# Turning tiles 0 to 3 once, with a copy kept by ScalarE, in an attention and gMLP mixer kernel

## The chip, the cores and the metric

The kernel runs on one core of a Trainium2 chip. The core has TensorE (PE, matrix products and transposes), VectorE (DVE), ScalarE (ACT), GpSimd (POOL) and SyncE (SP, which here issues DMAs). Each engine works through its own list of instructions in order; they meet only where one waits for another's result. TensorE writes its results to PSUM, a small memory of eight banks; a bank holds one tile of 128 x 512 fp32. The other working memory is SBUF. The metric is the device time of one execution in microseconds (us), the median of three.

## The reference

Input x is 2048 rows of 512. It is layer-normed to xn, and two branches read xn:

```python
s = attention(xn)      # 32 heads of 128; keys and values: the last 512 rows of a cache
z = gelu(xn @ w_in)    # 2048 x 1376, split in two halves of 688 columns
z1, z2 = z[:, :688], layernorm(z[:, 688:])
g = w_sp @ z2 + b_sp   # mixes the 2048 rows
out = x + s * silu((z1 * g) @ w_out)
```

All of it is fp32. The kernel gets that accuracy from three products: an operand is split into a high part, rounded to the faster matmul format fp32r, and a low part, which is the rest; high times high, high times low and low times high are added up in PSUM. In what follows a "rest" is the subtraction that makes a low part.

## The kernel before

**Tiles.** The 2048 rows of x are 16 tiles of 128 rows by 512. The first half, tiles 0 to 7, is loaded at the start into an SBUF array called `sacc`; this document is about those eight tiles. Each is layer-normed in place and then turned: four TensorE transposes of 128 x 128 (L215, for tile 0 at L231) put the turned tile in one PSUM bank (`flip`). From that bank ScalarE copies the high parts in two halves (L233), and VectorE subtracts to get the low parts (the rests, L59). The parts of tiles 0 to 3 lie in the blocks `X[0][h, 0]`, those of tiles 4 to 7 in `X[0][h, 1]`, h being the half of the 512 columns.

**Tile sums.** The query projections of most heads multiply a 2 x 2 arrangement of blocks with seven products in place of eight, in Strassen's manner. For that they need four combinations T1 to T4 of the turned tiles p and p + 4, for p = 0 to 3. They are made in two steps. When tile i of 4 to 7 is turned, ScalarE also copies the first 256 columns of its bank over the tile itself in `sacc` (y, L237), and VectorE subtracts them from the second 256 columns (L244). Later, in loop steps -3 to 0, `t_sums(p)` turns tile p a second time into a fresh bank, and `row_sums` has VectorE form three more combinations from that bank and y (L250 to L252). One step after each, `t_split(p)` splits the four results: high parts on ScalarE (L263), low parts on GpSimd.

**Order of the work.** The order is written out by hand, and every engine keeps the order in which the program emits its instructions. A prologue (L677 to L722) norms and turns tiles 0 to 3 and multiplies tiles 0, 1 and 2 with the first two of the four blocks of `w_in` (344 columns each); each product lands in a PSUM bank, is copied out by ScalarE into one of two staging tiles (L380) and stored to memory with a DMA that ScalarE issues (L381). I call these the z1 copies and stores. Then comes a loop over steps t from -7 on. Steps -7 to -4 turn one tile each, 4 to 7 (`ln_flip`); norm tile 6 or 7 ahead of need (L200, steps -7 and -6); and multiply one more tile with a block of `w_in` (`FILL`). All early steps carry a piece of the first query projections. From step 0 on each step also computes a block of attention scores (`score`). Work put in the list `late` runs at the end of its step, on VectorE, after all else of that step. `todo` holds what a step does besides, `t_sums` and `t_split` among it.

**Buffers.** PSUM is two pools of four banks: `ps_step` for what lives within a step and `ps_acc` for accumulators. Before the change all eight tiles are turned into banks of `ps_step`. SBUF scratch tiles of 128 x 512 named `rawx` come from the pool `xq` (five of them), which nothing else uses before step 30.

Of the kernel before, what the change touches and what calls it, by code (L numbers as in the profile page):

```python
# [8 lines left out]
F32 = mybir.dt.float32  # L9
# [3 lines left out]
OP = mybir.AluOpType  # L13
# [4 lines left out]
P = 128  # L18
# [3 lines left out]
NC = D // P  # L22
# [18 lines left out]
def mixer_kernel(ctx: ExitStack, tc: tile.TileContext, x, wh, w_in, w_sp, b_sp, w_out, out):  # L41
# [8 lines left out]
    nc = tc.nc  # L50
# [7 lines left out]
    def rest(engine, lo, whole, hi):  # L58
        engine.tensor_tensor(lo, whole, hi.bitcast(F32), op=OP.subtract)  # L59

    late = []
# [21 lines left out]
    ps_acc = psum.enter_context(tc.tile_pool(name="ps_acc", bufs=4, space=PSUM))  # L83
    ps_step = psum.enter_context(tc.tile_pool(name="ps_step", bufs=4, space=PSUM))
# [6 lines left out]
    xq = att.enter_context(tc.tile_pool(name="xq", bufs=5))  # L91
    sacc = sp.tile([P, T8, D], F32, name="sacc")


    def x8(shape, dtype=F32R):
        return xp.tile(shape, dtype, name="x8")
# [57 lines left out]
    X = {0: {}, 1: {}}  # L154

    def block():
        return x8([P, 2, 2, 512])

    def quarter(t, j):
        return t[:, :, j * P:(j + 1) * P]  # L160
# [31 lines left out]
    def ln_open(i):  # L192
        a, b = next(g for g in GROUPS if g[0] <= i < g[1])
        if i == b - 1:
            ln_stats([sacc[:, j, :] for j in range(a, b)], a)

    def ln_apply(t, i):
        mean, r = rx[i]
        if i:
            nc.vector.scalar_tensor_tensor(t, t, mean, r.to_broadcast([P, D]), op0=OP.subtract, op1=OP.mult)  # L200
        else:
            for k in range(2):
                sl = t[:, k * (D // 2):(k + 1) * (D // 2)]
                nc.vector.tensor_scalar(sl, sl, mean, r, op0=OP.subtract, op1=OP.mult)
# [7 lines left out]
    def flip(t, late=False):  # L212
        ps = ps_acc.tile([P, NC, P], F32, name="ps_a") if late else ps_step.tile([P, NC, P], F32, name="ps_3")
        for c in range(NC):
            nc.tensor.transpose(ps[:, c, :], t[:, c * P:(c + 1) * P], ident)  # L215
        return ps

    def ln_flip(i, parts=1):
        n, j = divmod(i, 4)
        if j == 0:  # L220
            for h in range(2):
                X[0][h, n] = block()
        if parts == 1:
            ps = flip(sacc[:, i, :])
        else:
            ps = ps_step.tile([P, NC, P], F32, name="ps_3")
        rests, rest_of = [], []
        for h in range(2):
            if parts > 1:
                for c in (2 * h, 2 * h + 1):  # L230
                    nc.tensor.transpose(ps[:, c, :], sacc[:, i, c * P:(c + 1) * P], ident)  # L231
            hi, lo = (quarter(X[0][h, n][:, a], j) for a in range(2))
            nc.scalar.copy(hi, ps[:, 2 * h:2 * h + 2])  # L233
            rests.append((lo, ps[:, 2 * h:2 * h + 2], hi))
        if n == 1:
            p2, y = ps.rearrange("p c q -> p (c q)"), sacc[:, i, :]
            nc.scalar.copy(y[:, :256], p2[:, :256])  # L237
            rest_of.append((y[:, 256:], p2[:, 256:], y[:, :256]))
        if parts > 1:
            return rests  # L240
        for r in rests:
            rest(nc.vector, *r)
        for r in rest_of:
            nc.vector.tensor_tensor(*r, op=OP.subtract)  # L244

    TS = ("T2", "T1", "T3", "T4")

    def row_sums(ps, y, o):

        nc.vector.tensor_tensor(o[:, :256], y[:, :256], ps[:, :256], op=OP.subtract)  # L250
        nc.vector.tensor_tensor(o[:, 256:], ps[:, :256], y[:, 256:], op=OP.add)
        nc.vector.tensor_tensor(y[:, :256], ps[:, 256:], o[:, 256:], op=OP.subtract)  # L252

    def t_sums(p):
        if p == 0:
            X[0].update((k, block()) for k in TS)
        row_sums(flip(sacc[:, p, :]).rearrange("p c q -> p (c q)"), sacc[:, 4 + p, :], sacc[:, p, :])

    def t_split(p):
        y, o = sacc[:, 4 + p, :], sacc[:, p, :]  # L260
# [110 lines left out]
    def z1_product(i, n, between=lambda: None):  # L371
        ps = ps_acc.tile([P, 512], F32, name="ps_a") if n or i >= T8 else ps_step.tile([P, 512], F32, name="ps_3")
        zmm(ps[:, :NB], i, n, range(2))
        between()
        zmm(ps[:, :NB], i, n, range(2, NC))
        return ps

    def z1_out(i, n, ps):
        z = zs.tile([P, NB], F32, name="z1")
        nc.scalar.copy(z, ps[:, :NB])  # L380
        nc.scalar.dma_start(z1_dram[:, i, n * NB:(n + 1) * NB], z)  # L381

    def z1_piece(i, n, between=lambda: None):
        z1_out(i, n, z1_product(i, n, between))
# [186 lines left out]
    def at(t, f, *args):  # L571
        todo.setdefault(t, []).append((f, args))
# [52 lines left out]
                q_events.setdefault(t0 + done + 2, []).append((q_done, g, k))  # L625

    for p in range(4):
        at(-3 + p, t_sums, p)
        at(-2 + p, t_split, p)
    ends = {}  # L630
    ends.setdefault(-2, []).append((keep_x, (0, 1)))
# [48 lines left out]
    low0 = split_piece(w0, 0, None, True), split_piece(w0, 1, None, True)  # L680
    ln_apply(rows[0], 0)
    low = ln_flip(0, 2)
    ln_open(1)
    for r in (*low0, *low):
# [4 lines left out]
    ps = ps_step.tile([P, 512], F32, name="ps_3")  # L689
    zmm_in(FIRST, ps[:, :NB], 0, 0, 0, 10)  # L690
    ln_open(2)
    ln_flip(1)
    zmm_in(FIRST, ps[:, :NB], 0, 0, 10, 12)
    low1 = [split_piece(w1, k, None, True) for k in range(4)]
# [3 lines left out]
    ps = ps_step.tile([P, 512], F32, name="ps_3")  # L698
# [6 lines left out]
    ps = ps_acc.tile([P, 512], F32, name="ps_a")  # L705
    zmm_in(THIRD, ps[:, :NB], 0, 1)
    ln_flip(2)
    ln_apply_late(3)
    ln_open(4)
# [4 lines left out]
    rest(nc.vector, *lowq)  # L714
    z1_out(0, 1, ps)
    z1_out(1, 1, ps1)
    ln_apply(rows[4], 4)
    ln_apply(rows[5], 5)
    z1_piece(2, 0)
    ln_open(6)  # L720
    ln_open(7)
    z1_piece(2, 1)  # L722

    FILL = dict(zip((-7, -6, -5, -4, -3, -2, -1, 0, 1, 8),
                    [(i, 1) for i in range(3, T8)] + [(i, 0) for i in range(4, T8)] + [(3, 0)]))
# [2 lines left out]
    for t in range(T0, T1):  # L728
# [6 lines left out]
        i = t + XL  # L735
# [23 lines left out]
        if t in DRAIN:  # L759
            ps = z1_product(*DRAIN[t])  # L760
# [21 lines left out]
    ps = z1_product(*LAST[-1])  # L782
# [422 lines left out]
```

## Time and profile before

| | us |
|---|---|
| Median of three runs | 1763.73 |
| Lowest and highest | 1763.12, 1763.81 |
| The profiled execution | 1763.41 |
| Its span in the profile | 1761.6 |

| Engine | Busy, us | Instructions |
|---|---|---|
| TensorE, matmuls | 1754.7 | 8463 |
| TensorE, weight loads (beside the matmuls) | 1506.7 | 8463 |
| VectorE | 1491.0 | 2470 |
| GpSimd | 1226.6 | 1151 |
| ScalarE | 1186.7 | 2621 |

The prologue and steps -7 to 0 take the first 46 us of the span. Rows of the profile name a line of the kernel, an engine, an operation and tiles as "out<-in"; "x4" merges four in a row; text in brackets is how long the engine had been idle before, and whose result it waited for. Matmuls are pipelined: the recorded time of one overlaps the next, so what a matmul holds of TensorE is the distance from its start to the next start. ACTq rows are DMAs that ScalarE issues; they take time on ScalarE's list though they do not count as busy.

### The profile page before, as it was taken

The numbers are of one execution on the slowest core, as the hardware profiler recorded it, in microseconds if no ns is written. First come the engines' busy times: TensorE is split into PE (matmuls) and PEld (weight loads), VectorE is DVE, ScalarE is ACT, GpSimd is POOL, SyncE is SP. The second block draws the span as 40 slices with busy tenths as digits, with TensorE's granted clock in tenths as the row PEclk, the third lists the DMA queues.
The fourth block names the chain that finished last, engine by engine and source line by source line (L and its number), as shares of the span: only waits on it lengthen the run. The fifth ranks groups of instructions, "written<-read, shape, count | busy, mean of one in ns | idle before, by whom it ended". The sixth has DMA issues, their size and how long they took to land.

```text
span 1761.6 us, 28515 instructions
## 1 busy us (share of the span) xinstructions
PE 1754.7 (100%) x8463; PEld 1506.7 (86%) x8463; DVE 1491.0 (85%) x2470; ACT 1186.7 (67%) x2621; POOL 1226.6 (70%) x1151
## 2 busy tenths in 40 slices
PE   9999999999999999999999999999999999999999
PEld 8888888888888888888888888888888899999997
DVE  6789989898998989988888888888888647887875
ACT  5777777777777777777777777777777546543333
POOL 2889888888888889878888888888888411000032
PEclk9999999999999999999999999999999999999999
DMA  5688887888888889787887877877788652655496
GB/s 203 209 236 253 247 248 233 248 240 236 251 241 239 250 231 272 217 262 223 224 224 221 229 227 220 226 222 219 232 226 247 216 194 86 224 187 177 148 257 206
DMA packets 171708, 394.25 MB, mean 224 GB/s; under 512 B 23840, under 2 KB 53792, under 8 KB 152352
## 3 DMA queue, kind: packets, MB, share of 16 engines
q1 hardware_dynamic: 166944, 386.80, 74.8%
q10 hardware_dynamic: 4608, 5.64, 0.9%
q8 instruction: 66, 1.08, 0.3%
q14 instruction: 90, 0.74, 0.1%
HBM read 229.55 MB, written 162.79 MB: 223 GB/s over the span
## 4 chain that ended last, share of the span: by engine, by line
PE 98%; DMA 1%; DVE 0%; ACT 0%; issue 0%; SPq 0%; ACTq 0%
PE ps_a L473 17%; PE ps L65 13%; PE ps L67 13%; PE ps L66 13%; PE ps L906 11%; PE ps_a L540 6%; PE ps_a L539 6%; PE ps_a L538 6%; PE ps_a L67 2%; PE ps_a L66 2%; PE ps_a L65 2%; PE ps_f L67 1%; PE ps_f L66 1%; PE ps_f L65 1%; PE ps_f L906 1%; DMA pL<-p_dram 1%
## 5 line engine op out<-in xcount | busy, mean ns | idle before, releaser
L59 POOL TENSOR_TENSOR pT_l<-pL,pT_h 128x512 fp32r<-128x512 f32 x507 | 658.0, 1301 | 185.1 <-ACT pT_h L530 176.1
L502 ACT ACTIVATE prob<-ps,nm 128x512 f32<-128x512 f32 x512 | 354.0, 691 | 339.7 <-DVE nm L500 331.6
L562 DVE SCALAR_TENSOR_TENSOR sacc<-ps,sums,sacc 128x512 f32<-128x512 f32 x496 | 369.8, 746 | 119.2 <-PE ps L67 114.0
L473 PE MATMUL ps_a<-x,x 128*128 128x512 f32 x1266 | 365.3, 389 | 0.0
L511 DVE STREAM_TRANSPOSE pL<-prob 128x512 f32<-128x512 f32 x512 | 358.8, 701 | 0.5 <-ACT prob L502 0.4
L500 DVE TENSOR_REDUCE nm<-ps 128x1 f32<-128x512 f32 x512 | 340.3, 665 | 3.0 <-PE ps L67 2.9
L530 ACT CAST pT_h<-pL 128x512 fp32r<-128x512 f32 x512 | 318.4, 622 | 9.2 <-ACT z L380 4.2
L473 PEld LDWEIGHTS ps_a<-x,x 128*128 128x128 f32 x1266 | 237.7, 188 | 49.2 <-issue 0.2
L59 POOL TENSOR_TENSOR wl<-raw,wh 128x512 fp32r<-128x512 f32 x186 | 241.7, 1299 | 10.9 <-ACT wh L145 10.9
L65 PE MATMUL ps<-wh,qT_h 128*128 128x512 f32 x512 | 199.7, 390 | 0.3 <-DVE sacc L562 0.2
L538 PE MATMUL ps_a<-pT_h,wh 128*128 128x512 f32 x512 | 199.9, 390 | 0.0
L67 PE MATMUL ps<-wh,qT_l 128*128 128x512 f32 x512 | 199.6, 390 | 0.0
L540 PE MATMUL ps_a<-pT_l,wh 128*128 128x512 f32 x512 | 199.4, 389 | 0.0
L65 PE MATMUL ps<-wh,oT_h 128*128 128x512 f32 x512 | 199.3, 389 | 0.0
L66 PE MATMUL ps<-wl,qT_h 128*128 128x512 f32 x512 | 199.3, 389 | 0.0
L539 PE MATMUL ps_a<-pT_h,wl 128*128 128x512 f32 x512 | 199.3, 389 | 0.0
L67 PE MATMUL ps<-wh,oT_l 128*128 128x512 f32 x512 | 199.2, 389 | 0.0
L66 PE MATMUL ps<-wl,oT_h 128*128 128x512 f32 x512 | 199.2, 389 | 0.0
L906 PE MATMUL ps<-b,x 128*128 128x344 f32 x1248 | 191.8, 316 | 0.0
L906 PEld LDWEIGHTS ps<-b,x 128*128 128x128 f32 x1248 | 191.5, 188 | 0.0
L59 POOL TENSOR_TENSOR b<-b 128x512 fp32r<-128x512 f32 x2 | 2.5, 1292 | 189.5 <-DMA x<-s_dram 189.5
L59 POOL TENSOR_TENSOR x<-wq,x 128x256 fp32r<-128x256 f32 x177 | 131.1, 741 | 0.0
(216 smaller groups left out, 3039.5 us busy)
## 6 DMA issues: line engine op xcount, KB each, us to landing
p_dram<-pL SPq DMA_DIRECT2D x128, 1024.0 KB, 4.7
pL<-p_dram SPq DMA_DIRECT2D x256, 192.0 KB, 4.0
raw<-wh SPq DMA_DIRECT2D x188, 256.0 KB, 6.1
pL<-p_dram SPq DMA_DIRECT2D x256, 128.0 KB, 4.0
x<-w_sp SPq DMA_DIRECT2D x24, 1024.0 KB, 5.1
pL<-p_dram SPq DMA_DIRECT2D x256, 64.0 KB, 3.9
wq<-wh SPq DMA_DIRECT2D x60, 256.0 KB, 5.6
z_dram<-z ACTq DMA_DIRECT2D x32, 172.0 KB, 3.3
```

Of the source, the lines that this page charges most:

```text
L59: engine.tensor_tensor(lo, whole, hi.bitcast(F32), op=OP.subtract)
L65: nc.tensor.matmul(ps, lh, rh, start=first, stop=False)
L66: nc.tensor.matmul(ps, lh, rl, start=False, stop=False)
L67: nc.tensor.matmul(ps, ll, rh, start=False, stop=last)
L473: nc.tensor.matmul(qps[g, bank], wt["q", g, k][a][:, c * P:(c + 1) * P], X[g * 2 // H][ORDER[k]][:, b, c], start=first, stop=r == 5, skip_ ...
L500: nc.vector.tensor_reduce(nm, ps, axis=AX.X, op=OP.max, negate=True)
L502: nc.scalar.activation(prob[t], ps, AF.Exp, bias=nm, accum_out=sums[b][:, j:j + 1])
L511: nc.vector.transpose(pL[b][:, :, j * P:j * P + P].rearrange("p a (c q) -> p a c q", q=Q), prob.pop(t).rearrange("p (a c q) -> p a c q", a ...
L530: nc.scalar.copy(h, p)
L538: nc.tensor.matmul(pps[b], vh, ph, start=c == 0, stop=False)
L562: nc.vector.scalar_tensor_tensor(at, ps, rs, at, op0=OP.mult, op1=OP.add)
L906: nc.tensor.matmul(ps, a, b, start=k != "P4" and c == 0 and m == 0, stop=c == RP - 1 and m == 2, skip_group_check=True)
```

## The change

Tiles 0 to 3 are turned only once, in the prologue. The bank of each is kept until ScalarE has copied it whole into a `rawx` tile (`keep_whole`): the copy of tile 0 stands after the z1 copies of tiles 0 and 1, that of tile 1 in the middle of the next product, those of tiles 2 and 3 in the middle of the one after. In ScalarE's list this is: two z1 copies, copy 0, copy 1, z1 copy, copy 2, copy 3, z1 copy. Tiles 0 and 1 are turned into banks of `ps_acc` now.

The combinations are formed when tile p + 4 is turned, in steps -7 to -4: `ln_flip` puts `row_sums` into `late`, four subtractions that read the bank of tile p + 4 and the kept copy of tile p. So the bank of tile p + 4 stays in use until the end of its step, and the four subtractions of a pair stand together. The second turning and the old sums in steps -3 to 0 are gone; what is left at step -3 allocates the blocks for T1 to T4. `t_split` stays where it was. DMAs are neither added nor removed.

```diff
+    def keep_whole(i):
+        p2, whole[i] = whole[i], xq.tile([P, 512], F32, name="rawx")
+        nc.scalar.copy(whole[i], p2)
...
         if parts == 1:
-            ps = flip(sacc[:, i, :])
+            ps = flip(sacc[:, i, :], i == 1)
         else:
-            ps = ps_step.tile([P, NC, P], F32, name="ps_3")
-        rests, rest_of = [], []
+            ps = ps_acc.tile([P, NC, P], F32, name="ps_a")
+        rests = []
...
+        p2 = ps.rearrange("p c q -> p (c q)")
         if n == 1:
-            p2, y = ps.rearrange("p c q -> p (c q)"), sacc[:, i, :]
+            y = sacc[:, i, :]
             nc.scalar.copy(y[:, :256], p2[:, :256])
-            rest_of.append((y[:, 256:], p2[:, 256:], y[:, :256]))
+            late.append((row_sums, p2, y, sacc[:, i - 4, :], whole[i - 4]))
+        whole[i] = p2
...
-    def row_sums(ps, y, o):
-
-        nc.vector.tensor_tensor(o[:, :256], y[:, :256], ps[:, :256], op=OP.subtract)
-        nc.vector.tensor_tensor(o[:, 256:], ps[:, :256], y[:, 256:], op=OP.add)
-        nc.vector.tensor_tensor(y[:, :256], ps[:, 256:], o[:, 256:], op=OP.subtract)
-
-    def t_sums(p):
-        if p == 0:
-            X[0].update((k, block()) for k in TS)
-        row_sums(flip(sacc[:, p, :]).rearrange("p c q -> p (c q)"), sacc[:, 4 + p, :], sacc[:, p, :])
+    def row_sums(ps, y, o, x):
+
+        for to, x0, x1 in ((y[:, 256:], ps[:, 256:], y[:, :256]), (o[:, :256], ps[:, :256], x[:, :256]),
+                           (o[:, 256:], ps[:, 256:], o[:, :256]), (y[:, :256], x[:, 256:], o[:, 256:])):
+            nc.vector.tensor_tensor(to, x0, x1, op=OP.subtract)
+
+    def t_blocks():
+        X[0].update((k, block()) for k in TS)
...
     for p in range(4):
-        at(-3 + p, t_sums, p)
+        if p == 0:
+            at(-3, t_blocks)
         at(-2 + p, t_split, p)
...
     z1_out(1, 1, ps1)
+    keep_whole(0)
     ln_apply(rows[4], 4)
     ln_apply(rows[5], 5)
-    z1_piece(2, 0)
+    z1_piece(2, 0, lambda: keep_whole(1))
     ln_open(6)
     ln_open(7)
-    z1_piece(2, 1)
+    z1_piece(2, 1, lambda: (keep_whole(2), keep_whole(3)))
```

More of the change, by code (lines that the diff above doesn't have):

```diff
@@ L216, in flip @@
         return ps
+    whole = {}
+    def keep_whole(i):
+        p2, whole[i] = whole[i], xq.tile([P, 512], F32, name="rawx")
+        nc.scalar.copy(whole[i], p2)
     def ln_flip(i, parts=1):
@@ L242, in ln_flip @@
             rest(nc.vector, *r)
-        for r in rest_of:
-            nc.vector.tensor_tensor(*r, op=OP.subtract)
     TS = ("T2", "T1", "T3", "T4")
-    def row_sums(ps, y, o):
-        nc.vector.tensor_tensor(o[:, :256], y[:, :256], ps[:, :256], op=OP.subtract)
-        nc.vector.tensor_tensor(o[:, 256:], ps[:, :256], y[:, 256:], op=OP.add)
-        nc.vector.tensor_tensor(y[:, :256], ps[:, 256:], o[:, 256:], op=OP.subtract)
-    def t_sums(p):
-        if p == 0:
-            X[0].update((k, block()) for k in TS)
-        row_sums(flip(sacc[:, p, :]).rearrange("p c q -> p (c q)"), sacc[:, 4 + p, :], sacc[:, p, :])
+    def row_sums(ps, y, o, x):
[4 more added lines that the diff above has]
+        X[0].update((k, block()) for k in TS)
     def t_split(p):
```

## The prediction

> **What bounds the kernel now.** I read the page first: the busy times and the chain that ended last.
>
> ```profile
> span 1761.6 us, 28515 instructions
> PE 1754.7 (100%) x8463; PEld 1506.7 (86%) x8463; DVE 1491.0 (85%) x2470; ACT 1186.7 (67%) x2621; POOL 1226.6 (70%) x1151
> PE 98%; DMA 1%; DVE 0%; ACT 0%; issue 0%; SPq 0%; ACTq 0%
> ```
>
> TensorE is the bound: busy for 1754.7 of 1761.6 us and 98% of the chain. A busy TensorE can still hide waits, so I asked next what it waited for, over the whole span:
>
> ```profile
> PE ps L673 <- POOL ident masks.py:199: 1.3, 1, 1.3
> PE ps L231 <- ACT x L233: 0.5, 1, 0.5
> PE ps L368 <- DVE pT_l L59: 0.3, 1, 0.3
> PE ps L65 <- DVE sacc L562: 0.2, 1, 0.2
> ```
>
> Four waits, 2.3 us in all, and none near the code that changes. So TensorE work that is taken out shortens the run by what it holds of TensorE's time, unless a new wait takes its place. The rest of the working is therefore TensorE's timeline around the change, and the timelines of ScalarE and VectorE beside it.
>
> **What is removed on TensorE.** The loop steps -3 to 0 each begin with a second turning of one of tiles 0 to 3 (four 128x128 transposes at L215). First the group over the whole span and in the window 33.2 to 43 us, then TensorE's timeline; its columns are start, duration, engine, line.
>
> ```profile
> L215 PE MATMUL ps<-ident,sacc x44: 271/272/328, 9.6 to 42.7; 128*128 128x128 f32 x44
> ...
> L215 PE MATMUL ps<-ident,sacc x16: 271/272/273, 33.2 to 42.7; 128*128 128x128 f32 x16
> 33.25 0.60 PE L215 MATMUL ps<-ident,sacc 128*128 128x128 f32 x4
> 33.60 0.40 PE L65 MATMUL ps_a<-wh,x 128*128 128x344 f32 x1
> 33.84 0.32 PE L66 MATMUL ps_a<-wl,x 128*128 128x344 f32 x1
> 34.00 0.32 PE L67 MATMUL ps_a<-wh,x 128*128 128x344 f32 x1
> 42.33 0.60 PE L215 MATMUL ps<-ident,sacc 128*128 128x128 f32 x4
> ```
>
> All 16 of these go. A recorded duration (272 ns) is not what a transpose holds, since neighbours overlap: four of them occupy TensorE from 33.25 to the next start at 33.60, 0.35 us. The matmul behind them then takes 0.24 us to the next start (33.60 to 33.84) where its neighbour takes 0.16 (33.84 to 34.00), so the switch costs another 0.08. One turning is worth 0.43 to 0.44 us, four are worth **1.75 us**. No transpose is added: tiles 0 to 7 are turned in the prologue and in steps -7 to -4 as before.
>
> [...]
>
> **What is added on ScalarE.** Four copies of a whole turned tile, 128x512 from PSUM. The same operation stands later in this kernel, and around the new place ScalarE's timeline reads:
>
> ```profile
> L320 ACT COPY rawx<-ps_a x8: 578/578/580, 166.8 to 571.5; 128x512 f32<-128x512 f32 x8
> 18.59 0.33 ACTq L381 DMA_DIRECT2D z_dram<-z  x1
> 18.95 0.45 ACT L380 COPY z<-ps_a 128x344 f32<-128x344 f32 x1 [0.40 <-ACT z L380]
> 19.43 0.33 ACTq L381 DMA_DIRECT2D z_dram<-z  x1
> 20.47 0.45 ACT L380 COPY z<-ps 128x344 f32<-128x344 f32 x1 [1.07 <-DMA z_dram<-z]
> 21.37 0.45 ACT L380 COPY z<-ps_a 128x344 f32<-128x344 f32 x1 [0.45 <-PE ps_a L67]
> 22.22 0.65 ACT L233 CAST x<-ps 128x256 fp32r<-128x256 f32 x2 [0.40 <-ACT z L380]
> 22.75 0.39 ACT L237 COPY sacc<-ps 128x256 f32<-128x256 f32 x1
> 24.80 0.65 ACT L233 CAST x<-ps 128x256 fp32r<-128x256 f32 x2 [0.69 <-PE ps L215]
> 26.70 0.45 ACT L380 COPY z<-ps_a 128x344 f32<-128x344 f32 x1 [0.97 <-PE ps_a L67]
> ```
>
> The copies cost 4 x 0.58 = 2.3 us of ScalarE, less an overlap of about 0.09 each (two casts of 0.37 take 0.65 together). I laid them out in program order. The z1 store issue at 19.43 ends at 19.76. Copy 0 runs from 19.79 to 20.37, copy 1 to 20.86. The z1 copy now at 20.47 follows at 20.77, its store issue ends at 21.58, copies 2 and 3 run to 22.68, the z1 copy now at 21.37 moves to 22.59, and its store issue ends at 23.40. Tile 4's casts, now at 22.22, start at 23.43: **ScalarE is 1.2 us late there**. The idle time at 24.80 and 26.70 absorbs it: tile 5's casts come 0.3 us late (the z1 copy between ends at 24.71, its store issue at 25.07), and the copy at 26.70 is on time again. The only DMAs moved are those three z1 stores, 0.3 to 1.2 us later; the pair of staging tiles has them landed again by about 25.3 (1.9 us after issue: the copy at 20.47 waits for the store at 18.59), before the copy at 26.70 wants one.
>
> Who waits for tile 4's casts? VectorE's rests, and behind them TensorE's product of tile 4.
>
> **What moves on VectorE.** The 16 small subtractions stay 16 (four per pair of tiles), but 12 move from steps -3 to 0 into steps -7 to -4, where each group stands at the end of its step, ahead of the next tile's rests.
>
> ```profile
> 23.17 0.76 DVE L59 TENSOR_TENSOR x<-ps,x 128x256 fp32r<-128x256 f32 x2 [0.28 <-ACT sacc L237]
> 23.85 0.41 DVE L244 TENSOR_TENSOR sacc<-ps,sacc 128x256 f32<-128x256 f32 x1
> 24.18 0.74 DVE L200 SCALAR_TENSOR_TENSOR sacc<-sacc,mv,rs_r 128x512 f32<-128x512 f32 x1
> 25.76 0.76 DVE L59 TENSOR_TENSOR x<-ps,x 128x256 fp32r<-128x256 f32 x2 [0.84 <-ACT sacc L237]
> 31.81 0.76 DVE L59 TENSOR_TENSOR x<-ps,x 128x256 fp32r<-128x256 f32 x2 [1.94 <-ACT sacc L237]
> 34.23 0.69 DVE L775 SCALAR_TENSOR_TENSOR qT_l<-ps_a,qT_h 128x512 fp32r<-128x512 f32 x1 [1.33 <-ACT qT_h L400]
> 34.84 0.41 DVE L250 TENSOR_TENSOR sacc<-sacc,ps 128x256 f32<-128x256 f32 x1
> 35.17 0.42 DVE L251 TENSOR_TENSOR sacc<-ps,sacc 128x256 f32<-128x256 f32 x1
> 35.62 0.42 DVE L252 TENSOR_TENSOR sacc<-ps,sacc 128x256 f32<-128x256 f32 x1
> ```
>
> An independent subtraction follows after 0.33 us (34.84 to 35.17), one that reads its predecessor after 0.45 (35.17 to 35.62). The new four have two such dependences: 0.33 + 0.45 + 0.45 + 0.33 = 1.56 us. A step with rests (0.68), a layer-norm apply (0.66) and sums (1.56) fills 2.90 us of VectorE; the steps without the apply take 2.24. TensorE's step is 3.03 us (33.25 to 42.33 is three of them). VectorE keeps pace, with little to spare.
>
> The consumers are the third matmul of each tile's product, which reads the first rest (24.92, 27.95, 30.97; the row at 19.25 is for the next part):
>
> ```profile
> 19.25 0.32 PE L65 MATMUL ps_a<-wh,x 128*128 128x344 f32 x1
> ...
> 24.52 0.40 PE L65 MATMUL ps_a<-wh,x 128*128 128x344 f32 x1
> 24.92 0.32 PE L67 MATMUL ps_a<-wh,x 128*128 128x344 f32 x1
> 27.95 0.32 PE L67 MATMUL ps_a<-wh,x 128*128 128x344 f32 x1
> 30.97 0.32 PE L67 MATMUL ps_a<-wh,x 128*128 128x344 f32 x1
> ```
>
> Tile 4: the rests start once ScalarE's last copy of the bank has ended, as the row at 23.17 shows, so at 24.38; the first ends at 24.80, wanted at 24.92. Tile 5: rests 24.38, apply 25.06, sums 25.72 to 27.28, next rests 27.28, first done 27.70, wanted 27.95. Tile 6: 30.18, done 30.60, wanted 30.97. Tile 7: 32.42, done 32.84, wanted after 33.6. Every margin is positive, the tightest 0.12 us. I take **no stall**, and keep 0 to 1.0 us: at the lower end the margins hold; at the upper all of ScalarE's added 2.3 us arrives at tile 4's first rest, which had 1.33 us in hand (it ends at 23.17 + 0.42, the time of one such operation, = 23.59, and is wanted at 24.92).
>
> [...]
>
> **New claims on buffers.** Turned tiles 0 to 3 hold a PSUM bank until their copy. Tiles 0 and 1 now draw from the pool of accumulators, and the product of tile 2 with the second weight block, which starts at 19.25, is its fifth allocation. If buffers went strictly round, it would take tile 0's bank and wait for copy 0. The rows above say otherwise: the product at 33.60 is the ninth allocation of that pool and would take the bank of the fifth, which VectorE reads until 34.92; it didn't wait. Banks go by order of release, and the first released are those of the two z1 copies before the store issues at 18.59 and 19.43. So no wait: 0, with 1.17 us as the upper end (copy 0's end at 20.37, plus 0.05 for the signal, less 19.25).
>
> **Does the gain survive?** From step 0 on TensorE only reaches its later work 1.75 us sooner. GpSimd is the busiest helper there:
>
> ```profile
> 40.86 1.31 POOL L59 TENSOR_TENSOR wl<-raw,wh 128x512 fp32r<-128x512 f32 x1 [0.93 <-ACT wh L145]
> 53.68 1.30 POOL L59 TENSOR_TENSOR wl<-raw,wh 128x512 fp32r<-128x512 f32 x1 [1.74 <-ACT wh L145]
> ```
>
> It works without a gap from 40.86 to 51.93. That stretch starts about 0.9 us earlier (two turnings precede it), so it ends at 51.05; the next request comes at 51.93. TensorE has only the 0.2 us wait behind it. The gain stays, and if GpSimd were late it could take back at most the 1.75.
>
> **Sum.** -1.75 + 0 + 0 = -1.75 us: the profiled run of 1763.41 us (span 1761.6 and 1.8 around it) becomes 1761.7, and the median of 1763.73, which lies 0.3 above that run, becomes **1762.0**.
>
> **Rivals.**
> 1. Strictly round buffers: TensorE loses 1.17 us at 19.25 and gains 0.58 net, 1763.1. Against it speaks 33.60.
> 2. Late rests: one stall of up to 1.0 us in steps -6 to -4, 1762.1 to 1763.0. For it speaks the margin of 0.12; against it, that a delay of TensorE widens every later margin.
> 3. The gain is given back to GpSimd or to loads between 43 and 70 us: no change, 1763.7. Against it, TensorE's empty list of waits there.
> 4. Slower: VectorE becomes the bound of steps -7 to -4. It decides where a new subtraction costs over 0.63 us in place of 0.39 (the long steps then take 3.86 us and the short ones 3.20, and two long and one short lose 2 x 0.83 + 0.17, less the margin of 0.12: the gain). At the most a row allows, the 0.69 of an operation twice as wide (34.23), the long steps take 4.10 and the short ones 3.44: 2 x 1.07 + 0.41 - 0.12 = 2.4 lost, +0.7 net, 1764.4. Against it, 0.33 to 0.45 in the rows.
> 5. Each transpose is worth its recorded duration: 16 x 0.272 = 4.35 us, 1759.4. Against it, four in 0.35 us. [...]
>
> **How the numbers follow.** My forecast has a chance of 0.68; the rivals 0.09, 0.11, 0.05, 0.04 and 0.03. The forecast's own range, with 0.3 us of spread between runs, is 1761.7 to 1762.4. Rivals 1 and 2 stretch the range up to 1763.5; 1761.0 below leaves room for a turning that holds about 0.2 us more than I read. About 0.2% (3.5 us) is what a measurement of this kernel tells from no change: faster is below 1760.2, slower above 1767.3. Only rival 5 is surely faster, and I add 0.01; rival 4 as priced stays within, so slower has 0.03 for a cause that I don't see, and 0.93 is left for the same.
>
> **What would show it.** After the change: 28 transposes of L215 instead of 44 before 43 us; the L215 rows gone between steps -3 and 0, with TensorE steps of about 2.6 us there; the wait list of TensorE as before; tile 4's casts at about 23.4 us and its rests at 24.4; VectorE without subtractions of tile sums after 36 us; the first score matmul, now 0.35 us after 42.33, at about 40.9. A TensorE wait on a ScalarE copy at 19.25 is rival 1, one on L59 between 24.9 and 31 is rival 2 or 4. A first score at 40.9 with a total unchanged is rival 3.

## The result, and the profile after

The changed kernel takes **1775.09 us** (median of 6 runs, 1774.00 to 1775.67) against 1763.77 us for the kernel before (6 runs, 1763.12 to 1764.40). The ratio is 1.0065 with a 95% interval of 1.0055 to 1.0075: **slower by 11.3 us**, where 1762.0 was predicted. The profiled execution took 1775.42 us, with a span of 1773.6. One run of experiment 8 below took 2197.6 us at a granted clock of 0.753 and is not counted; every other run lies at 0.997 to 1.000.

The page of the changed kernel, span and busy times:

```profile
span 1773.6 us, 28485 instructions
PE 1762.5 (99%) x8447; PEld 1514.3 (85%) x8447; DVE 1491.6 (84%) x2470; ACT 1188.2 (67%) x2625; POOL 1226.3 (69%) x1151
```

TensorE issues 16 instructions fewer, as it should, and yet is busy for 7.8 us longer (1762.5 against 1754.7) and idle for 4.2 us more (11.1 against 6.9). So there are two losses, idle time and work that takes longer. The list of TensorE's waits names the first:

```profile
PE ps L912 <- ACT b L826: 4.1, 1, 4.1
PE ps L678 <- POOL ident masks.py:199: 1.3, 1, 1.3
...
PE ps_a L67 <- DVE x L59: 0.2, 1, 0.2
```

The last row, 0.2 us, is dealt with further below. One wait of 4.1 us is new: L912 for L826. (Lines below the edit have moved: L912 is L906 of the kernel before, L826 is L820, L258 stands in place of L244 and L250 to L252.) L912 is the row mixing, the product with `w_sp`: 1344 matmuls of 344 columns that start some 1450 us after the changed code. L826 is the gelu of the last z products, the stage just before. TensorE's timeline there, first of the kernel before, then of the changed one (columns: start, duration, engine, line, in brackets the idle time before):

```profile
1489.00 0.32 PE L67 MATMUL ps_a<-raw,x 128*128 128x344 f32 x1
1489.15 22.24 PE L906 MATMUL ps<-b,x 128*128 128x344 f32 x144
1511.23 1.08 PE L906 MATMUL ps_f<-b,x 128*128 128x344 f32 x6
```

```profile
1488.01 0.31 PE L67 MATMUL ps_a<-raw,x 128*128 128x344 f32 x1
1492.41 25.60 PE L912 MATMUL ps<-b,x 128*128 128x344 f32 x144 [4.09 <-ACT b L826]
1517.85 7.42 PE L912 MATMUL ps_f<-b,x 128*128 128x344 f32 x46
```

Until 1488 us the changed kernel is ahead by 0.99 us (1489.00 less 1488.01). Then it waits for the last gelu. Before, the row mixing did not: ScalarE's timelines of the kernel before and the changed one show that the same gelu ran at 1492.55 there, 3.4 us after the row mixing had begun.

```profile
1492.55 0.80 ACT L820 ACTIVATE b<-ps_a 128x344 f32<-128x344 f32 x2
```

```profile
1489.04 1.81 ACT L847 ACTIVATE b<-b,rz_r 128x688 f32<-128x688 f32 x2 [2.61 <-POOL rz_r L841]
1490.88 0.77 ACT L853 CAST b<-b 128x688 fp32r<-128x688 f32 x1
1491.56 0.80 ACT L826 ACTIVATE b<-ps_a 128x344 f32<-128x344 f32 x2
```

The wait is not all. The next table has the granted clock by stretches (columns: stretch, its length, then busy time and count of PE, PEld, DVE, ACT and POOL, the granted TensorE clock, DMA share, GB/s); the changed kernel first, then the last stretch for the kernel before.

```profile
1491.40:1498.30 6.90, 5.89 (x21) 5.89 (x22) 6.44 (x12) 5.75 (x10) 1.58 (x2) 0.51 0.01 2
...
1520.00:1600.00 80.00, 80.00 (x509) 80.00 (x508) 62.30 (x73) 35.01 (x41) 0.00 (x0) 1.00 0.59 194
```

```profile
1520.00:1600.00 80.00, 80.00 (x523) 80.00 (x523) 65.96 (x77) 35.47 (x41) 0.00 (x0) 1.00 0.61 206
```

For 6.9 us, from 1 us before the end of the wait, the clock is granted at 0.51, and only 21 matmuls start. And then, with the clock at 1.00 again, TensorE still does less: 509 matmuls in 80 us against 523, 2.7% fewer, with no wait between them. This lasts to the end of the row mixing. The groups of the row mixing (columns: count, shortest, median and longest duration in ns, first and last start) say the same, before and after:

```profile
L906 PE MATMUL ps<-b,x x1248: 316/316/316, 1489.2 to 1695.1; 128*128 128x344 f32 x179
```

```profile
L912 PE MATMUL ps<-b,x x1248: 316/320/652, 1492.4 to 1707.0; 128*128 128x344 f32 x179
```

I call the two spacings the short and the long pace: 0.153 us from start to start (1489.15 to 1511.23 is 144 of them) and 0.158 (below). In a group of this stage a median of 316 ns marks the short, 320 the long one.

**Account.** The first row-mixing matmul is 3.26 us late (1492.41 less 1489.15): 4.25 lost, 0.99 in hand. The first 144 take 25.44 us instead of 22.08, 3.36 more: about 2.7 at half clock (21 matmuls in 5.89 us of work, where 38 would start at the short pace), the rest already the long pace. The other 1200 lose 5.3 (the last one starts at 1707.0 against 1695.1, 11.9 late): the long pace. The sum is 11.9 us; the spans differ by 12.0.

### The profile page after: what moved, and what is told of

Read it like the earlier page. It is cut to its first block, busy times and chain, and to the rows that moved or that the text cites. A ratio compares the mean times of both kernels' runs of the same rounds, so it can differ in the third digit from the quotient of the medians.

```text
span 1773.6 us, 28485 instructions
## 1 busy us (share of the span) xinstructions
PE 1762.5 (99%) x8447; PEld 1514.3 (85%) x8447; DVE 1491.6 (84%) x2470; ACT 1188.2 (67%) x2625; POOL 1226.3 (69%) x1151
## 4 chain that ended last, share of the span: by engine, by line
PE 96%; DMA 2%; ACT 1%; DVE 1%; POOL 0%; issue 0%; DVEq 0%; ACTq 0%; POOLq 0%; SPq 0%
PE ps_a L477 16%; PE ps L65 13%; PE ps L67 13%; PE ps L66 13%; PE ps L912 11%; PE ps_a L544 6%; PE ps_a L543 6%; PE ps_a L542 6%; PE ps_a L67 2%; PE ps_a L66 2%; PE ps_a L65 2%; PE ps_f L65 1%; PE ps_f L66 1%; PE ps_f L67 1%; PE ps_f L912 1%; DMA pL<-p_dram 1%
## 5 line engine op out<-in xcount | busy, mean ns | idle before, releaser
L912 PE MATMUL ps<-b,x 128*128 128x344 f32 x1248 | 200.1, 322 | 4.1 <-ACT b L826 4.1
L912 PEld LDWEIGHTS ps<-b,x 128*128 128x128 f32 x1248 | 199.6, 190 | 4.4 <-ACT b L826 4.4
```

What stands on the lines that cost most here:

```text
L912: nc.tensor.matmul(ps, a, b, start=k != "P4" and c == 0 and m == 0, stop=c == RP - 1 and m == 2, skip_group_check=True)
```

## Where the wait comes from

Every PSUM tile is given a bank when the program is built; of the banks that are free a pool takes the one released first. The pools `ps_step` and `ps_acc` are closed before the row mixing, and a new pool starts, whose tiles named "ps" get the banks 0, 5, 4, 3, 2, 1, in that order, whatever came before. The built programs give these banks to the last z products, in the order of the program:

```
before:  ... ps_a 0, ps_3 5, ps_3 4, ps_a 2, ps_a 3   | row mixing: 0, 5, 4, ...
after:   ... ps_a 3, ps_3 6, ps_3 5, ps_a 2, ps_a 0   | row mixing: 0, 5, 4, ...
```

The change takes six tiles fewer from `ps_step` (the four second turnings, and tiles 0 and 1) and two more from `ps_acc`, and it holds some of them longer. That turns the order in which banks come free, and nothing between there and 1488 us turns it back. The last z product, whose gelu is the last to run, now lies in the very bank that the row mixing takes first.

**Theory A**: the whole loss comes from this; the moved work itself gains what was predicted. **Rival B**: the moved work shifts ScalarE's or GpSimd's later work, and the wait would be there with any banks. **Rival C**, on the second part of the loss: the long pace is a matter of the clock, or of the length of the idle time.

## The experiments

All times are medians; the kernel before, measured beside each experiment, took 1763.46 to 1763.55 us. Short diffs are against the changed kernel unless said otherwise.

**1. The change with another bank order.** One line: the tile of the warm-up transposes, whose contents nothing reads, comes from the other pool.

```diff
-    warm = ps_step.tile([P, NC, P], F32, name="ps_3")
+    warm = ps_acc.tile([P, NC, P], F32, name="ps_a")
```

> The changed kernel with one allocation moved: the tile of the warm-up transposes comes from ps_acc instead of ps_step. No instruction is added or removed; only the order in which the accumulator banks go round is shifted, so that the last product before the row mixing lands in bank 3 as in the kernel before, and the first row-mixing product takes a bank that has long been free. Theory (the loss is TensorE's 4.1 us wait for the last gelu at the start of the row mixing, because that product's bank is reused first, and what follows from the wait): no such wait, granted clock 1.00, the matmuls of the row mixing 0.153 us apart as before, and 1762.8 us (1762.2 to 1763.3), below the kernel before by the 0.8 to 1.0 us that TensorE is ahead before 1480 us. Rival A (ScalarE is late there through the added copies, whatever the bank): the wait stays, about 1775. Rival B (the 3% slower matmuls come from the change itself, not from the wait): no wait but 0.158 us apart, about 1768.

Measured: 1762.01 us (11 runs, 1761.73 to 1762.36), ratio 0.9992 (0.9983 to 1.0001). The last z product lies in bank 3 again. Row mixing in this kernel, by TensorE's timeline and by groups:

```profile
1487.69 22.24 PE L912 MATMUL ps<-b,x 128*128 128x344 f32 x144
...
L912 PE MATMUL ps<-b,x x1248: 316/316/316, 1487.7 to 1693.6; 128*128 128x344 f32 x179
```

No wait, no half clock, short pace. The work of the change is all there, and 13.1 us are gone. B falls: the banks alone make the wait. (All 11 runs lie below the 15 of the kernel before, 1763.10 to 1764.01, but the interval of the ratio reaches 1.0001.)

**2. The kernel before with turned banks.** No work is changed, only the pool from which three tiles come (against the kernel before):

```diff
-            ps = flip(sacc[:, i, :])
+            ps = flip(sacc[:, i, :], i == 1)
...
-            ps = ps_step.tile([P, NC, P], F32, name="ps_3")
+            ps = ps_acc.tile([P, NC, P], F32, name="ps_a")
...
-    warm = ps_step.tile([P, NC, P], F32, name="ps_3")
+    warm = ps_acc.tile([P, NC, P], F32, name="ps_a")
```

> The kernel before with three allocations moved to ps_acc (the warm-up transposes' tile and the turned tiles 0 and 1) and nothing else: no copy is kept, the second turning stays. The last product before the row mixing then lands in bank 0, which the first row-mixing product takes. Theory: the whole loss appears without the change: a wait of about 4.1 us on the gelu, 6.8 us of half clock, matmuls 3% slower to the end of the row mixing; 1763.8 + 4.2 + 3.4 + 5.3 = 1776.7 us (1775.5 to 1777.5). Rival A (the loss needs the kept copies or the moved sums): 1763.8.

Measured: 1775.56 us (5 runs, 1775.27 to 1776.62), ratio 1.0070 (1.0057 to 1.0083). In TensorE's waits and groups the whole picture of the changed kernel appears:

```profile
PE ps L906 <- ACT b L820: 4.1, 1, 4.1
...
L906 PE MATMUL ps<-b,x x1248: 317/320/656, 1494.0 to 1708.2; 128*128 128x344 f32 x179
```

**3. The kernel before with tiles 0 and 1 in the other pool** (the first two edits of experiment 2, without the warm-up tile), which is the part of the change that concerns the allocation in the prologue.

> The kernel before with the turned tiles 0 and 1 in ps_acc: the one part of the change that only moves allocations. The last product of the first 344-column half of the last tile lands in bank 0; its gelu ends some 0.35 us before that of the second half. Theory: a wait of about 3.7 us at the start of the row mixing. If that is enough for the clock to fall, 1776 us; if not, and the slower matmuls belong to the fall of the clock, 1767.5 us; if not, and they belong to any wait, 1773. Rival A (the loss needs the kept copies or the moved sums): 1763.8.

Measured: 1774.72 us (4 runs, 1773.99 to 1774.81), ratio 1.0063 (1.0049 to 1.0076). Bank 0 now holds the first half of the last tile, whose gelu ends one earlier: the wait is 3.7 us instead of 4.1, and the half clock 3.4 us long (1493.6 to 1497.0). The long pace is the same.

```profile
PE ps L906 <- ACT b L820: 3.7, 1, 3.7
...
1492.83 7.47 PE L906 MATMUL ps<-b,x 128*128 128x344 f32 x36 [3.73 <-ACT b L820]
```

So the three losses are one chain that starts with a bank. The next five kernels take the chain apart: they are the changed kernel, wait and all, with unused matmuls or transposes added, whose results nothing reads.

**4. Work in the wait: 26 unused matmuls** of 344 columns after the last z product.

```diff
+    fill = ps_step.tile([P, 512], F32, name="ps_3")
+    for k in range(26):
+        nc.tensor.matmul(fill[:, :NB], x_op(ZO[-1], k % 2, k % NC), wt[("w", 3), k % NC][0][:, :NB], start=True, stop=True)
```

> The changed kernel with 26 more matmuls of 344 columns (about 4.0 us) between the last product and the first row-mixing product; their result goes to a free bank and is not used. They stand where TensorE only waits. Theory (half of the loss is the wait, the rest the clock that falls because TensorE is idle): the first row-mixing product still starts at about 1492.4 us, the clock stays at 1.00, the matmuls after it are 0.153 us apart, and the time is 1763.8 - 1.0 + 4.25 = 1767.0 us. Rival C (the slower matmuls after it come from the bank or from the change, not from idle time): 1772 to 1775. Rival D (the wait isn't idle time that can be filled): 1779.

Measured: 1772.76 us (4 runs, 1772.34 to 1773.05), ratio 1.0052 (1.0038 to 1.0066): **a miss** by 5.8 us. The clock stayed at 1.00, but the pace is long all the same. TensorE's timeline shows what is left of the wait:

```profile
1492.02 0.47 PE L988 MATMUL ps<-wh,x 128*128 128x344 f32 x2
1492.59 22.99 PE L912 MATMUL ps<-b,x 128*128 128x344 f32 x144
1515.41 7.74 PE L912 MATMUL ps_f<-b,x 128*128 128x344 f32 x48
```

The last unused matmul ends at 1492.49, the first product starts at 1492.59. That is a break of 0.1 us, and 144 matmuls take 22.82 us, 0.1585 each. My expectation, that the pace followed from the half clock, is refuted, and with it the half of rival C that names the clock.

**5. 32 unused matmuls**, so that no break is left; and **6. 13 of them**, so that half of the wait is left.

> The changed kernel with 32 instead of 26 unused matmuls of 344 columns (4.9 us) before the first row-mixing product, so that they end after the last gelu and TensorE doesn't wait at all. With 26 of them the wait was down to about 0.1 us and the clock held, and yet the row mixing stayed 3% slow. Theory (any break in the stream, however short, leaves this weight-load-bound stage in a slower pace that lasts to its end): no break, 0.153 us apart, and 0.9 us more work makes the kernel 5 us faster than with 26: 1762.0 + 4.9 = 1766.9 us (1766.3 to 1767.6). Rival (the slower pace comes from the bank, or from the unused matmuls, not from the break): still 0.158 us apart, 1773.6.

> The changed kernel with 13 unused matmuls (2.0 us), so that about 2.1 us of the wait are left. Theory (a short wait doesn't lower the clock, but brings the slow pace): clock 1.00, 0.158 us apart, the same 1772.8 us as with 26 unused matmuls. Rival (2 us are enough for the clock to fall): 1775 to 1776, about as without any.

Measured with 32: 1767.22 us (10 runs, 1766.42 to 1767.62), ratio 1.0020 (1.0011 to 1.0030). Measured with 13: 1773.04 us (4 runs, 1772.67 to 1773.12), ratio 1.0054 (1.0040 to 1.0068). First the kernel with 32, then the one with 13:

```profile
1491.82 0.47 PE L988 MATMUL ps<-raw,x 128*128 128x344 f32 x2
1492.13 22.24 PE L912 MATMUL ps<-b,x 128*128 128x344 f32 x144
```

```profile
PE ps L912 <- ACT b L826: 2.1, 1, 2.1
...
L912 PE MATMUL ps<-b,x x1248: 317/320/428, 1492.7 to 1704.7; 128*128 128x344 f32 x179
```

Six unused matmuls more than in experiment 4 make the kernel 5.5 us faster. A break of 0.1 us and one of 2.1 us were followed by the same pace (144 matmuls from 1492.59 and from 1492.66, 22.99 us in both), so the other half of rival C falls too: in these two runs the length of the idle time made no difference to the pace. After 2.1 us of idle time the clock stayed at 1.00 (stretch 1491.40 to 1498.30 with 13 unused matmuls).

**7. Transposes in the wait**, 44 unused ones of 128x128 in place of the matmuls.

> The kernel after, with 44 unused 128x128 transposes of the identity (about 0.089 us apart, 3.9 us) on TensorE in the 4.1 us wait ahead of the row mixing, in place of the 26 unused matmuls. Theory A (transposes hold the clock as matmuls do; the warm-up of the changed kernel, 24 transposes alone, was granted the full clock while it ran): clock 1.00 throughout, slow pace through the row mixing because a switch or a gap of some 0.1 us or more breaks the stream, total as with the 26 matmuls, 1772.0 to 1773.5 us. Theory B (transposes do not count as work for the clock): the granted clock falls to 0.5 for 3.4 to 6.8 us from about 1491 to 1495, total 1774.0 to 1775.7 us.

Measured: 1773.15 us (4 runs, 1772.72 to 1773.39), ratio 1.0055 (1.0038 to 1.0071). Theory A of that expectation holds: the clock is 1.00 throughout. The transposes started 0.109 us apart (4.96 us for 44, the last one recorded with 0.27), not 0.089. The pace is long here too (median 320 ns), although the profile shows no idle time at all (PE busy 20.00 of 20.00 us): in this run the long pace followed the transposes as it followed the breaks. The rows are from TensorE's timeline, the groups of the row mixing and the table of stretches.

```profile
1487.92 4.96 PE L988 MATMUL ps<-ident 128*128 128x128 f32 x44
...
L912 PE MATMUL ps<-b,x x1248: 314/320/402, 1492.6 to 1704.6; 128*128 128x344 f32 x179
...
1480.00:1500.00 20.00, 20.00 (x144) 19.98 (x143) 17.03 (x31) 16.21 (x24) 3.41 (x4) 1.00 0.31 95
```

**8. A stretch of other matmuls**: the wait is left as it is, and 12 unused matmuls of 512 columns stand ahead of the fifth row-mixing product.

```diff
         step(t)
+        if t == 4:
+            lead = pp.tile([P, 512], F32, name="ps_f")
+            for k in range(12):
+                nc.tensor.matmul(lead, ops[t][:, 0, k % RP], ops[t][:, 0].rearrange("p c t -> p (c t)")[:, :512], start=True, stop=True)
```

> The changed kernel, its wait left in place, with 12 unused matmuls of 512 columns (2.7 us) ahead of the fifth row-mixing product. Theory (the slow pace is lost lead of the weight loads over the matmuls; matmuls of 512 columns, which outlast a weight load, let the lead come back): 0.158 us apart before them and 0.153 after, 1775.1 + 2.7 - 5.2 = 1772.6 us. Rival (the slow pace is a state of the clock or lasts for a time): 0.158 to the end, 1777.8.

Measured: 1771.58 us (3 runs, 1770.54 to 1771.59), ratio 1.0044 (1.0029 to 1.0060). By TensorE's timeline and the stretches of the granted clock:

```profile
1492.70 16.74 PE L912 MATMUL ps<-b,x 128*128 128x344 f32 x96 [4.08 <-ACT b L826]
1509.28 2.92 PE L1147 MATMUL ps_f<-x 128*128 128x512 f32 x12
...
1492.30:1495.70 3.40, 3.00 (x10) 3.00 (x11) 3.23 (x8) 2.61 (x4) 1.26 (x2) 0.50 0.02 5
1513.00:1600.00 87.00, 87.00 (x569) 87.00 (x568) 67.09 (x79) 38.58 (x46) 0.00 (x0) 1.00 0.59 194
```

After the 12 matmuls the pace is short, to the end: 569 in 87 us is 0.153 each. The kernel beats the expectation by 1.0 us, which has the size of the shorter half clock: it lasted 3.4 us here, not 6.9, after the same wait. The forecast of the pace came true, but its reason, a lost lead of the weight loads, is not shown: a weight load starts 0.15 us before its matmul in the short pace (kernel before) and 0.16 in the long one (changed kernel). That a matmul of 512 columns outlasts a weight load is in the rows: a load of the row mixing is recorded with 0.188 us, and such matmuls start 0.227 us apart (9 from 1371.39 to 1373.43 in the kernel before).

**9. The best version.** Experiment 1, and beside it the splitting of a block of weights is moved from step -5 to step -3: its low part, which GpSimd makes at 29.74 in the changed kernel, and the cast on ScalarE ahead of it (why, see below).

```diff
-    at(-5, lambda: split_piece(("h", 0), 1, nc.gpsimd))
+    at(-3, lambda: split_piece(("h", 0), 1, nc.gpsimd))
```

> The kernel with the bank order repaired, and the split of the first key piece moved from step -5 to step -3, so that GpSimd doesn't read SBUF while VectorE forms the fourth tile sum, which has both inputs in SBUF. In the changed kernel that sum took 1.11 us instead of 0.42, and TensorE waited 0.19 us for the rest behind it and lost about 0.4. Theory (the two share a way to SBUF): the fourth sums all take 0.42, TensorE doesn't wait on a rest, 1762.0 - 0.4 = 1761.6 us. Rival (the long sum comes from something else): it stays long, 1762.0.

Measured: 1761.83 us (11 runs, 1761.50 to 1762.19), ratio 0.9991 (0.9982 to 1.0000). Its median is 1.7 us below the kernel before and 0.2 below experiment 1. Both are the change as it was meant; by the bound of 0.2% neither can be told from no change, and the 0.2 us between them is not shown.

## Why the prediction was wrong, point by point

**What is removed: right.** Of the L215 rows before 43 us 28 are left, 24 and 4:

```profile
L215 PE MATMUL ps<-ident,sacc x24: 271/272/273, 14.9 to 30.9; 128*128 128x128 f32 x24
...
L215 PE MATMUL ps_a<-ident,sacc x4: 271/272/273, 10.0 to 10.3; 128*128 128x128 f32 x4
```

TensorE's steps are shorter as forecast; its timeline repeats the 512-column product of the step at 35.97 and 38.56, 2.59 us (forecast about 2.6):

```profile
35.97 0.39 PE L65 MATMUL ps_a<-x,wh 128*128 128x512 f32 x1
...
38.56 0.39 PE L65 MATMUL ps_a<-x,wh 128*128 128x512 f32 x1
```

At 1488 us experiment 1 is 1.46 us ahead of the kernel before (1489.15 less 1487.69), and its median 1.45. The forecast gain was 1.75; the late rest below, 0.44 us, is of the size of what is missing (experiment 9, without it, gains 1.7). That 1762.01 falls on the predicted 1762.0 is partly luck: the kernel before stood at 1763.46 beside it, not at 1763.73. Rival 5, at 4.35, is refuted: the recorded 0.272 us of a transpose is not its price in a stream.

**ScalarE: right.** The copies, and tile 4's casts, stand where the working put them, 0.3 us later because the whole prologue is:

```profile
20.12 1.07 ACT L222 COPY rawx<-ps_a 128x512 f32<-128x512 f32 x2 [0.40 <-ACT z L384]
21.95 1.07 ACT L222 COPY rawx<-ps 128x512 f32<-128x512 f32 x2 [0.40 <-ACT z L384]
23.77 0.65 ACT L239 CAST x<-ps 128x256 fp32r<-128x256 f32 x2 [0.40 <-ACT z L384]
```

The forecast was 19.79 and 23.43. The prologue started late on this run since the full clock was granted at 6.6 us, not 5.6 (the start of the first clock record in each trace; the table of stretches counts the time before it as 1.00). The warm-up transposes start 0.213 us apart before that moment and 0.109 after it (kernel before), and the 24 of them took 5.38 us, not 4.88 (rows of before and after):

```profile
1.34 4.88 PE L673 MATMUL ps<-ident 128*128 128x128 f32 x24 [1.34 <-POOL ident masks.py:199]
```

```profile
1.34 5.38 PE L678 MATMUL ps<-ident 128*128 128x128 f32 x24 [1.34 <-POOL ident masks.py:199]
```

The warm-up took between 4.24 us (32 unused matmuls) and 5.38 us in the eleven profiles of this study, with no order that I see: 5.38 in the kernel before with turned banks too, which has none of the change's work. So I take it for spread and not for the change.

**VectorE: one price wrong.** Four subtractions at 0.33, 0.45, 0.45 and 0.33 were forecast, and all but one came so. VectorE's timeline of tile 5's step, and GpSimd's beside it:

```profile
28.96 0.42 DVE L258 TENSOR_TENSOR sacc<-ps,sacc 128x256 f32<-128x256 f32 x1
...
29.74 0.42 DVE L258 TENSOR_TENSOR sacc<-ps,sacc 128x256 f32<-128x256 f32 x1
30.20 1.11 DVE L258 TENSOR_TENSOR sacc<-rawx,sacc 128x256 f32<-128x256 f32 x1
31.24 0.74 DVE L59 TENSOR_TENSOR x<-ps,x 128x256 fp32r<-128x256 f32 x2
```

```profile
29.74 1.29 POOL L59 TENSOR_TENSOR wl<-raw,wh 128x512 fp32r<-128x512 f32 x1 [5.75 <-DVE sacc L258]
```

The fourth subtraction reads both operands from SBUF. It took 1.11 us in place of 0.42 and ended at 31.31, shortly after GpSimd's operation (29.74 + 1.29 = 31.03). That used up the margin, and TensorE lost 0.44 us: its third matmul came 0.74 after the first instead of 0.40, and the next 0.26 later instead of 0.16 (24.52, 24.92 and 33.84, 34.00 in the prediction's rows).

```profile
30.96 0.40 PE L65 MATMUL ps_a<-wh,x 128*128 128x344 f32 x1
31.70 0.42 PE L67 MATMUL ps_a<-wh,x 128*128 128x344 f32 x1 [0.19 <-DVE x L59]
31.96 0.32 PE L65 MATMUL ps_a<-wh,x 128*128 128x344 f32 x1
```

This is rival 2 in its effect, by another cause than the one it named. With GpSimd's operation moved away (experiment 9) all four take the normal time; the cast that moved with it had ended at 29.66, before the long subtraction began:

```profile
L258 DVE TENSOR_TENSOR sacc<-rawx,sacc x4: 424/424/426, 27.0 to 34.4; 128x256 f32<-128x256 f32 x4
```

**The first score** came at 41.84 instead of 40.9, ahead of before by 0.84 and not by 1.75. The prologue has 0.3 of the difference and the late rest 0.44; for some 0.15 I have no row, and by 1488 us the lead was 0.99.

**"New claims on buffers" is the step that failed.** It asked whether the new order of banks makes TensorE wait in the prologue, found from the rows that banks go by order of release, and put the cost at 0. There it was right: no wait stands at 19.25, and rival 1 fell. But the same finding should have led on. If banks go by release, a changed number of allocations turns the order for the rest of the kernel. Within a pool that cost nothing here: no new wait for a bank stands in TensorE's list before 1488 us. It is not harmless where a pool is closed and the next hands out fixed banks, and there the step did not look. The cost taken as nothing was 4.25 us of wait, which drew some 9 us behind it.

**"Does the gain survive?"** looked at 43 to 70 us only. The lead did survive, to 1488 us, which is where it went. **The rivals**: the slower side was priced as a local stall of VectorE, 0.7 us above before; what came was 11.3, at another place. The prediction's own test, "the wait list of TensorE as before", is what shows it. That 0.03 were left for "a cause that I don't see" was far too little: a change that turns an order which the whole kernel inherits has as many places to go wrong as the order has users. One smaller reading was off as well: the prediction says that no wait of TensorE lies near the changed code, but the one at L231, 0.5 us, is in the turning of tile 0, whose pool changes; it stayed at 0.5 (L237 of the changed kernel).

## What to carry to other kernels

When a change adds, drops or moves a buffer, write down which physical bank or slot each later tile gets, in the program before and after, and look where a pool ends and another begins: the tile that is released last must not lie where the next stage starts. If an unrelated line at a far place suddenly waits, try the same work with one allocation more or less before you look for a cause in the work. And price a stall of TensorE by what follows it, not by its length: here 4.1 us of waiting cost 13 (1775.1 against 1762.0 in experiment 1).

## What the runs showed of the hardware

**Two paces at one clock.** In a stream of matmuls of 344 columns (weight-load engine busy 80 of 80 us) they start 0.153 or 0.158 us apart, both at a granted clock of 1.00. After breaks of 0.1, 2.1, 3.7 and 4.1 us ahead of the row mixing, and after 44 transposes without a break, the pace was long, and in the changed kernel it held for over 200 us (to 1707.0). After a stretch of 12 matmuls of 512 columns it was short again (experiment 8). The kernel before shows both by itself. Its timeline has one wait of 0.24 us:

```profile
1362.92 0.50 PE L65 MATMUL ps<-wh,qT_h 128*128 128x512 f32 x1 [0.24 <-DVE sacc L562]
```

The next matmuls of 344 columns start 0.158 us apart (1367.42 to 1369.16 is 11 of them); after 18 of 512 columns, those from 1373.43 on are 0.153 apart. The prologue and the early steps of the kernel before run at the long pace as well (33.84 to 34.00 in the prediction's rows is 0.16). In the profile with 32 unused matmuls, and in no other of this study, the early steps ran at the short one from 31.31 on, right behind a wait of 0.17 us, which I can't explain: there a break was followed by the short pace. What turns one pace into the other is open.

**The clock.** Idle times of 3.7 and 4.1 us were followed by half clock, one of 2.1 was not. The half clock lasted 3.4 us (experiments 3 and 8) or 6.8 (the changed kernel and experiment 2). By the clock records it came 2.2 us after the last matmul had ended in experiment 2 (1489.92 to 1492.12) and 3.1 us after it in the changed kernel (1488.32 to 1491.42); in experiment 3 it came at 1493.59, 0.8 us after the row mixing had begun, by the table of stretches:

```profile
1493.59:1497.01 3.42, 3.42 (x14) 3.42 (x14) 3.25 (x8) 2.27 (x4) 1.58 (x2) 0.50 0.00 0
```

What sets these lengths and moments is not shown. With 44 transposes in the place of the wait the clock stayed at 1.00 (1480 to 1500, experiment 7), where the same stretch of the changed kernel had 0.83. The warm-up is transposes alone, and the full clock was granted before the first matmul of another kind: at 5.57 us, before 7.09, in the kernel before, and at 6.63 us, before 7.62, in the changed kernel.

**VectorE beside GpSimd.** A subtraction of 128x256 with both inputs in SBUF took 1.11 us instead of 0.42 while GpSimd ran a subtraction (29.74 to 31.03); the one with one input in PSUM that ran beside the same operation took 0.42 (29.74). With GpSimd's operation moved away all four of the first kind took 0.42 (experiment 9). That the two share a way to SBUF, the theory of that expectation, is not shown: the runs show the times, not the cause.

**The two formats.** The section on the reference calls fp32r the faster matmul format; no run here makes the same product in both. At the full clock the fp32 transposes of 128 columns start 0.109 us apart (four recorded with 0.60 us, the last one with 0.27) and the fp32r matmuls of 512 columns 0.227.
